# A retention state updated with two heads per matmul, and weight units converted three steps later

## The chip, the cores and the metric

The kernel runs on one core of one Trainium2 chip. The metric is the device time of one execution in microseconds (us); a difference of 0.2% is 1.8 us here.

## The reference

Three stages run one after the other: a retention (attention with a decaying causal mask and no softmax) over 4 batches of 8 heads, 576 positions and 64 features per head; a two-layer block of width 2048 with the Mish activation; and a gated block of width 1536 with SiLU. Everything is float32.

```python
def _attn_ref(q, k, v):                       # (4, 8, 576, 64) each
    scores = scale * np.matmul(q, k.transpose(0, 1, 3, 2))
    gamma = 1.0 - 2.0 ** (-5.0 - np.arange(H, dtype=np.float32))
    Dmat = np.where(rel >= 0, gamma[:, None, None] ** rel[None, :, :], 0.0)
    return np.matmul(scores * Dmat[None], v)
...
x = attn_out.transpose(0, 2, 1, 3).reshape(B * S, H * D)    # (2304, 512)
h = x @ moe_w_in;  x = (h * np.tanh(np.log1p(np.exp(h)))) @ moe_w_out
g = x @ moe2_w_gate
out = (g * sigmoid(g) * (x @ moe2_w_val)) @ moe2_w_out
```

## The kernel before, in words

**Retention** (`retention`, L309 to L627) takes 20 steps: four batches, each cut into four pieces of 128 positions and a last one of 64 (`sc` counts the pieces, `nsc` is 5). The heads lie in four pairs (`NP`), `e` is the head within its pair. A step `t` is written out by hand, and every engine works through its instructions in the written order. On TensorE a step is: `inter` (L517), queries times the running state, into `o0` for the first 64 positions and `o1` for the second; `scores` (L457, in the short last piece L446); `state(t, 1)` (L498); `transposes(t + 1)` (L410, of the next keys); the matmuls of a slot of the next stage, in four of the steps; `products` (L530), the masked scores times the scaled values; `state(t + 1, 0)`; and `q_ahead`, transposes of queries (L379, in one step of five L372). The rows of the matmuls have 64 partitions and 64 columns: the float32 operands of the heads are laid on four quarters of the array (64 rows by 64 columns each).

**The state.** After each half `c` of 64 positions, `state(t, c)` adds k times v of that half to a state that stays in PSUM (`stp`, one tile per batch). For each of the eight heads there is one matmul of 64 by 64, which writes to the head's own half of the partitions; ScalarE then copies the state to SBUF (`sbd`, L507, 128 partitions by 256 elements), from where `inter` takes it as weights. There are 32 such updates (four batches, four full pieces, two halves).

**Around it.** ScalarE also copies the transposes out of PSUM (L381, L374, L412), VectorE masks the scores (L471) and scales the outputs into `x` (L540), GpSimd scales v (L427). Loads of k, v and q run four to six steps ahead (`load`, `load_q`).

**Weight units.** Each pair of weight blocks of the Mish layers is loaded raw (`fetch`, 512 KB) and turned into a high and a low part: `rebias_raw` (L106, L107), `sign` (L111), `join` (L115), `part` (L121 on ScalarE, L122 on GpSimd in retention and on VectorE after it). `conversions` yields these as pieces, in this order: rebias 0, sign 0, rebias 1, join 0, sign 1 with part 0, rebias 2, and so on. In retention `zeroth.one()` takes one piece per step from step 3 on (L611) and one more in each step listed in `EARLY` (L602). After retention each slot takes pieces worth `RATES[4]` = 3.3 (L740), where a unit's pieces are worth 0.55 + 1.4 + 0.7.

**EARLY slots.** The Mish layer's first four slots run inside retention, at the steps listed in `EARLY`: `g1` (L636, 12 matmuls) there, `mish` and its split one step later. Slots 0 and 1 read unit 0, slots 2 and 3 unit 1. `RATES` and `PREP` set how fast, and from which slot on, the pieces of the last stage's weights are handed out after retention (`second`, `third`).

Of the kernel before, what the change touches and what calls it, by code (L numbers as in the profile page):

```python
# [7 lines left out]
F32 = mybir.dt.float32  # L8
# [8 lines left out]
def retention_mish_swiglu(  # L17
# [17 lines left out]
    nc = tc.nc  # L35
    B, H, S, D = q.shape
# [4 lines left out]
    NP = H // 2  # L41
# [4 lines left out]
    C = 64  # L46
# [1 line left out]
    RAW, XS = 4, 6  # L48
    OFF = 2
    W = (12, 3, 8, 2, 2, 1)  # L50
    PREP = 25
    NC = 4
    RATES, AHEAD = (1.9, 1.2, 1.1, 1.15, 3.3), 45
    EARLY = (9, 11, 14, 17)

    xp = ctx.enter_context(tc.tile_pool(name="xp", bufs=1))
    cr = ExitStack()
# [253 lines left out]
    nsc = -(-S // 128)  # L311

    def retention(g1, mish, g_hi, g_lo):
        with ExitStack() as c0:
# [3 lines left out]
            at = c0.enter_context(tc.tile_pool(name="at", bufs=2))  # L318
            ps1 = c0.enter_context(tc.tile_pool(name="ps1", bufs=1, space=PSUM))
# [8 lines left out]
            sbd = {}  # L328
            qkv = {}
# [32 lines left out]
            qT, kT, vs, pp = {}, {}, {}, {}  # L362
# [23 lines left out]
            def q_cols(t):  # L386
                b, sc, n = steps[t]
                return qT[b, sc // 2][:, :, sc % 2 * 128:sc % 2 * 128 + n]


            def q_ahead(t, half):
                b, sc, n = steps[t]
                due = (
                    ((b, 1, 1),) if b else ((b, 1, 0),),
                    ((b, 2, 0),) if b else ((), (b, 1, 1)),
                    ((b + 1, 0, 0),) if b else ((b + 1, 0, 0), (b, 2, 0)),
                    ((b + 1, 0, 1),),
                    ((b + 1, 1, 0),),
                )[sc]
                if half < len(due) and due[half]:  # L400
                    q_transposes(*due[half])

            def transposes(t):
                if t >= len(steps):
                    return
                b, sc, n = steps[t]
                src = qkv["k", t]
                p = ps1.tile([128, NP, 128], F32, tag="tk", name=f"tk{t}")
                for pr in range(NP):
                    nc.tensor.transpose(p[:, pr, :n], src[:n, 2 * pr:2 * pr + 2, :], ident[:n, :n])  # L410
                kT[t] = at.tile([128, NP, 128], F32, tag="kT", name=f"kT{t}")
                nc.scalar.copy(out=kT[t][:, :, :n], in_=p[:, :, :n])  # L412
# [23 lines left out]
            def scores(t):  # L436
                if t >= len(steps):
                    return
                b, sc, n = steps[t]
                s = ps1.tile([128, 2, 512], F32, tag="s", name=f"s{t}")[:, :, :NP * C]  # L440
                s = s.rearrange("p e (a n) -> p e a n", a=NP)
                sc_[t] = s
                if n == C:
                    for pr in range(NP):
                        for e in range(2):
                            nc.tensor.matmul(  # L446
                                s[64 * e:64 * e + 64, 0, pr, :],
                                lhsT=kT[t][64 * e:64 * e + 64, pr, :C],
                                rhs=q_cols(t)[64 * e:64 * e + 64, pr, :],
                                start=True,  # L450
                                stop=True,
                            )
                    return
                for pr in range(NP):
                    for c in range(n // C):
                        for e in range(2):
                            nc.tensor.matmul(  # L457
                                s[C * c:C * c + C, e, pr, :],
                                lhsT=kT[t][64 * e:64 * e + 64, pr, C * c:C * c + C],
                                rhs=q_cols(t)[64 * e:64 * e + 64, pr, C * c:C * c + C],  # L460
                                start=True,
                                stop=True,
                            )

            def masks(t):
                if t >= len(steps):
                    return
                n, s = steps[t][2], sc_.pop(t)
                r = n // C
                pp[t] = at.tile([128, 2, NP, C], F32, tag="p", name=f"p{t}")  # L470
                nc.vector.tensor_tensor(  # L471
                    out=pp[t][:, :r], in0=s[:, :r],
                    in1=mask.unsqueeze(1).unsqueeze(1).to_broadcast([128, r, NP, C]),
                    op=ALU.mult,
                )
# [10 lines left out]
            stp = {}  # L486
            due = []

            def state(t, c):
                if t >= len(steps) or steps[t][1] == nsc - 1:  # L490
                    return
                b, sc, n = steps[t]
                if (sc, c) == (0, 0):
                    stp[b] = ps1.tile([128, NP, D], F32, tag="st", name=f"state{b}")
                for pr in range(NP):
                    for e in range(2):
                        h = 2 * pr + e
                        nc.tensor.matmul(  # L498
                            stp[b][64 * e:64 * e + 64, pr, :],
                            lhsT=qkv["k", t][C * c:C * c + C, h, :],  # L500
                            rhs=vs[t][C * c:C * c + C, h, :],
                            start=(sc == 0 and c == 0 and pr == 0),
                            stop=(sc == nsc - 2 and c == 1),
                            skip_group_check=True,
                        )
                sbd[t, c] = at.tile([128, NP, D], F32, tag="sbd", name=f"sbd{t}_{c}", bufs=3)
                nc.scalar.copy(out=sbd[t, c], in_=stp[b])  # L507

            outs_ = {}
# [1 line left out]
            def inter(t):  # L511
                b, sc, n = steps[t]
                outs_[t] = [ps1.tile([128, NP, C], F32, tag=f"o{c}", name=f"o{t}_{c}") for c in range(n // C)]
                for c in range(n // C):
                    for pr in range(NP if sc or c else 0):
                        for e in range(2):
                            nc.tensor.matmul(  # L517
                                outs_[t][c][64 * e:64 * e + 64, pr, :],
                                lhsT=sbd[(t, 0) if c else (t - 1, 1)][64 * e:64 * e + 64, pr, :],
                                rhs=q_cols(t)[64 * e:64 * e + 64, pr, C * c:C * c + C],  # L520
                                start=(pr == 0), stop=False, skip_group_check=True,
                            )
# [50 lines left out]
            def warm(n):  # L573
                for _ in range(n):
                    nc.tensor.matmul(idle[:, :128], lhsT=zero, rhs=zero, start=True, stop=True)  # L575
# [10 lines left out]
            for t in range(len(steps)):  # L586
                if t < 2:
                    warm(W[3 + t])
                if t == len(steps) - 1:
                    g1(LAG, (0, KT // 2))  # L590
                inter(t)
                scores(t)
                state(t, 1)
                masks(t)
                transposes(t + 1)
                q_ahead(t, 1)
                warm(W[5] if t < 2 else 0)
                if t == len(steps) - 1:
                    g1(LAG, (KT // 2, KT))
                if t in EARLY:  # L600
                    g1(EARLY.index(t))
                    zeroth.one()  # L602
                products(t)
                state(t + 1, 0)
                q_ahead(t, 0)
                scale(t + 2)
                if t + 1 < nsc:
                    gout_chunk(t + 1)
                if t - 1 in EARLY:
                    mish(EARLY.index(t - 1))  # L610
                if t > 2:  # L611
                    zeroth.one()
                if t - 1 in EARLY:
                    g_hi(EARLY.index(t - 1))
                    g_lo(EARLY.index(t - 1), nc.gpsimd)
                if due:
                    split_x(xt, "x", *due.pop(0), nc.gpsimd)
                load(t + 4, "k", k)
                load(t + 4, "v", v)
                if t == 0:  # L620
                    load_q(4)
                    load_q(5)
                load_q(t + 6)
                if t in (1, 3, 5):
                    fetch()
            splits[0] = nc.vector
            fetch()  # L627
# [1 line left out]
    with tc.manual_schedule():  # L629
# [38 lines left out]
        def g1(s, part_=(0, KT)):  # L668
            b, i = where(s)
            if not part_[0]:  # L670
                hs[s] = bank(s)
            prod(hs[s], unit["in", i], "x", b, part_)
# [44 lines left out]
        def slot(s):  # L717
# [22 lines left out]
            zeroth(RATES[4])  # L740
            if s >= PREP and not (parts and s < 2 * F1):
                third(RATES[3])
# [487 lines left out]
```

## Time and profile before

| | us |
|---|---|
| three runs, median (lowest to highest) | 916.27 (915.99 to 917.32) |
| the profiled execution | 915.34 |
| its span, first to last instruction | 913.6 |
| TensorE busy in the span | 899.7 (98%) |
| VectorE, ScalarE, GpSimd busy | 547.0, 375.9, 47.7 |

What is predicted is the time of the runs; the profiled execution is 0.93 us below their median, and its time is 1.74 us over its span. PE is TensorE's matmuls, PEld its weight loads, which run under other matmuls. A float32 matmul of L498, L517, L457, L530 and L575 leaves two records of each kind, a transpose or a matmul of the later stages one.

### The profile page before, as it was taken

Reading aid. Unit: us, or ns where it says so; the run is one execution under the profiler, and the core shown is the slowest. Engines: PE = TensorE matmul, PEld = TensorE weight load, DVE = VectorE, ACT = ScalarE, POOL = GpSimd, SP = SyncE. Lnnn points to the kernel's source line nnn. Section 1 sums busy time; section 2 is a strip of 40 time slices with the busy share of each in tenths; the row PEclk is TensorE's granted clock in tenths of the full one; section 3 lists DMA queues with packets and bytes.
Section 4 is the critical chain, followed back from the end, with each engine's and each line's share of the span. In section 5 each row is a group of like instructions: output and inputs, shape, how many; then the busy total and the mean of one; then the engine's idle time right before and its main releaser. Section 6 shows DMA issues by size and latency. Waiting matters only on the chain.

```text
span 913.6 us, 17176 instructions
## 1 busy us (share of the span) xinstructions
PE 899.7 (98%) x6810; PEld 840.9 (92%) x6810; DVE 547.0 (60%) x1094; ACT 375.9 (41%) x787; POOL 47.7 (5%) x52
## 2 busy tenths in 40 slices
PE   8899999999999999999999999999999999999998
PEld 8788899999999999999999999999999999999997
DVE  3344487866878784667695666747444556444444
ACT  3665456644655554454464333323222223222222
POOL 2344200000000000000000000000000000000000
PEclk9999999999999999999999999999999999999999
DMA  8997245544787767589859666545644455644421
GB/s 184 240 225 184 71 140 159 164 127 167 248 289 254 263 226 259 165 274 334 280 189 359 194 206 206 174 155 177 204 161 161 162 161 163 215 156 160 160 93 70
DMA packets 125648, 177.68 MB, mean 194 GB/s; under 512 B 47104, under 2 KB 84608, under 8 KB 125568
## 3 DMA queue, kind: packets, MB, share of 16 engines
q1 hardware_dynamic: 124432, 176.45, 61.3%
q8 instruction: 54, 0.88, 0.4%
q10 hardware_dynamic: 1136, 0.13, 0.1%
q14 instruction: 26, 0.21, 0.1%
HBM read 133.04 MB, written 43.52 MB: 193 GB/s over the span
## 4 chain that ended last, share of the span: by engine, by line
PE 95%; DVE 2%; ACT 1%; issue 1%; DMA 1%; SPq 0%; DVEq 0%; ACTq 0%
PE t L887 28%; PE fa L1063 16%; PE h L636 14%; PE ea L925 7%; PE da L925 7%; PE te L887 6%; PE acc L680 6%; PE o L517 2%; PE state L498 2%; PE o L530 1%; PE tk L410 1%; PE idle L575 1%; PE tq L379 1%; PE s L457 1%; PE acc L900 1%
## 5 line engine op out<-in xcount | busy, mean ns | idle before, releaser
L887 PE MATMUL t<-y,su 128*128 128x384 f32 x1512 | 306.5, 338 | 0.5 <-DVE cv L894 0.5
L887 PEld LDWEIGHTS t<-y,su 128*128 128x128 f32 x1512 | 270.7, 188 | 24.2 <-DVE cv L894 1.8
L1063 PE MATMUL fa<-fu,g 128*128 128x512 f32 x648 | 189.9, 395 | 0.1
L636 PE MATMUL h<-xs,u 128*128 128x384 f32 x672 | 127.5, 336 | 0.2 <-ACT m L697 0.2
L1063 PEld LDWEIGHTS fa<-fu,g 128*128 128x128 f32 x648 | 118.4, 188 | 7.6 <-ACT g L1086 0.5
L636 PEld LDWEIGHTS h<-xs,u 128*128 128x128 f32 x672 | 115.6, 188 | 1.7 <-ACT m L697 0.3
L1086 ACT CAST g<-sg 128x384 fp32r<-128x384 f32 x72 | 36.9, 513 | 173.7 <-DVE sg L1122 120.4
L925 PE MATMUL ea<-ge,u 128*128 128x512 f32 (+1 forms) x384 | 76.0, 336 | 0.0
L925 PE MATMUL da<-g,u 128*128 128x512 f32 (+1 forms) x384 | 72.0, 336 | 0.1
L887 PE MATMUL te<-ye,eu 128*128 128x384 f32 x336 | 68.0, 337 | 0.0
L925 PEld LDWEIGHTS ea<-ge,u 128*128 128x128 f32 x384 | 61.8, 188 | 5.9
L925 PEld LDWEIGHTS da<-g,u 128*128 128x128 f32 x384 | 60.4, 188 | 7.1 <-DVE x L540 0.4
L1111 ACT ACTIVATE sg<-sg 128x384 f32<-128x384 f32 x54 | 28.4, 526 | 90.6 <-DVE sg L894 90.6
L1091 DVE TENSOR_TENSOR g<-sg,g 128x384 fp32r<-128x384 f32 x72 | 40.2, 558 | 40.6 <-ACT g L1086 40.6
L680 PE MATMUL acc<-g,u 128*128 128x384 f32 x336 | 63.1, 336 | 0.8 <-DVE y L690 0.8
L710 DVE TENSOR_TENSOR g<-m,g 128x384 fp32r<-128x384 f32 x60 | 33.4, 556 | 46.6 <-ACT g L706 46.6
L680 PEld LDWEIGHTS acc<-g,u 128*128 128x128 f32 x336 | 58.6, 188 | 1.3 <-DVE y L690 1.3
L887 PEld LDWEIGHTS te<-ye,eu 128*128 128x128 f32 x336 | 56.8, 188 | 2.2 <-DVE ve L894 0.3
L697 ACT ACTIVATE m<-h 128x384 f32<-128x384 f32 x64 | 31.4, 490 | 55.3 <-PE h L636 55.0
L894 DVE TENSOR_TENSOR u<-t,p 128x384 f32<-128x384 f32 x36 | 20.0, 556 | 43.3 <-PE t L887 40.8
L894 DVE TENSOR_TENSOR v<-t,p 128x384 f32<-128x384 f32 x36 | 20.0, 556 | 35.6 <-PE t L887 34.9
L706 ACT CAST g<-m 128x384 fp32r<-128x384 f32 x64 | 32.9, 513 | 1.8
(131 smaller groups left out, 1039.6 us busy)
## 6 DMA issues: line engine op xcount, KB each, us to landing
su<-comb SPq DMA_DIRECT2D x126, 512.0 KB, 3.3
comb<-c SPq DMA_DIRECT2D x84, 256.0 KB, 2.6
eu<-ecomb SPq DMA_DIRECT2D x28, 512.0 KB, 4.6
raw<-in_moe_w_in_dram SPq DMA_DIRECT2D x16, 512.0 KB, 3.7
raw<-in_moe_w_out_dram SPq DMA_DIRECT2D x16, 512.0 KB, 3.7
ecomb<-e_s SPq DMA_DIRECT2D x32, 256.0 KB, 2.3
rawg<-in_moe_w_gate_dram SPq DMA_DIRECT2D x12, 512.0 KB, 6.1
ecomb<-u SPq DMA_DIRECT2D x24, 256.0 KB, 4.0
```

Source lines behind the costliest of these rows:

```text
L636: nc.tensor.matmul(ps, lhsT=u[:, a, kk * 128:(kk + 1) * 128], rhs=s[:, e, :], start=(c == 0), stop=(c == n - 1),)
L680: nc.tensor.matmul(accs[b][d][:, :T], lhsT=u[:, a, d * 128:(d + 1) * 128], rhs=g[:, e, :], start=(i == 0 and c == 0), stop=(i == F1 - 1 an ...
L697: nc.scalar.activation(w, hs.pop(s), AF.Mish)
L706: nc.scalar.copy(out=gs[s][:, 0, :], in_=ws[s])
L710: eng.tensor_tensor(out=g[:, 1, :], in0=ws.pop(s), in1=g[:, 0, :].bitcast(F32), op=ALU.subtract)
L887: nc.tensor.matmul(p, lhsT=w[:, a, kk * 128:(kk + 1) * 128], rhs=y[kk][:, x, :], start=begin and kk == 0 and (a, x) == (0, 0), stop=kk == ...
L894: nc.vector.tensor_tensor(out=out_, in0=a, in1=b_, op=ALU.add)
L925: nc.tensor.matmul(o, lhsT=u[:, a, d * 128:(d + 1) * 128], rhs=y[:, :512] if r == 0 else y[:, 512:], start=f == 0 and (a, x) == (0, 0) and ...
L1063: nc.tensor.matmul(accs["f", b][m], lhsT=gs[u, e, h][:, x, m * 128:(m + 1) * 128], rhs=fu[2 * (u % PAIRS) + e][:, a, :], start=first, stop ...
L1086: nc.scalar.copy(out=gs[u, e, h][:, 0, :], in_=x)
L1091: nc.vector.tensor_tensor(out=g[:, 1, :], in0=x, in1=g[:, 0, :].bitcast(F32), op=ALU.subtract)
L1111: nc.scalar.activation(x, bank_ if part_ is None else x, AF.Silu)
```

## The change

The state tile gets a full bank of PSUM, 128 columns per pair of heads. `state` takes both heads of a pair at once: the weights are the keys of both (64 rows by 128 columns), the moving operand is the values of both (128 columns), and the result holds the two heads' states on its diagonal and two products of unlike heads beside it, which nothing reads. The copy to `sbd` takes the whole bank, 128 by 512 elements, and `inter` reads the diagonal blocks. The pieces of the weight units start at step 6 instead of 3, the three raw loads of the loop come at steps 4, 6 and 8 instead of 1, 3 and 5, and the EARLY slots stand at steps 11, 13, 15 and 17 instead of 9, 11, 14 and 17. `PREP` and two of the `RATES` are a little higher.

```diff
--- before.py
+++ after.py
@@ -48,10 +48,10 @@
     RAW, XS = 4, 6
     OFF = 2
     W = (12, 3, 8, 2, 2, 1)
-    PREP = 25
+    PREP = 26
     NC = 4
-    RATES, AHEAD = (1.9, 1.2, 1.1, 1.15, 3.3), 45
-    EARLY = (9, 11, 14, 17)
+    RATES, AHEAD = (1.95, 1.2, 1.15, 1.15, 3.3), 45
+    EARLY = (11, 13, 15, 17)
 
     xp = ctx.enter_context(tc.tile_pool(name="xp", bufs=1))
     cr = ExitStack()
@@ -491,19 +491,17 @@
                     return
                 b, sc, n = steps[t]
                 if (sc, c) == (0, 0):
-                    stp[b] = ps1.tile([128, NP, D], F32, tag="st", name=f"state{b}")
+                    stp[b] = ps1.tile([128, NP, 128], F32, tag="st", name=f"state{b}")
                 for pr in range(NP):
-                    for e in range(2):
-                        h = 2 * pr + e
-                        nc.tensor.matmul(
-                            stp[b][64 * e:64 * e + 64, pr, :],
-                            lhsT=qkv["k", t][C * c:C * c + C, h, :],
-                            rhs=vs[t][C * c:C * c + C, h, :],
-                            start=(sc == 0 and c == 0 and pr == 0),
-                            stop=(sc == nsc - 2 and c == 1),
-                            skip_group_check=True,
-                        )
-                sbd[t, c] = at.tile([128, NP, D], F32, tag="sbd", name=f"sbd{t}_{c}", bufs=3)
+                    nc.tensor.matmul(
+                        stp[b][:, pr, :],
+                        lhsT=qkv["k", t][C * c:C * c + C, 2 * pr:2 * pr + 2, :],
+                        rhs=vs[t][C * c:C * c + C, 2 * pr:2 * pr + 2, :],
+                        start=(sc == 0 and c == 0 and pr == 0),
+                        stop=(sc == nsc - 2 and c == 1),
+                        skip_group_check=True,
+                    )
+                sbd[t, c] = at.tile([128, NP, 128], F32, tag="sbd", name=f"sbd{t}_{c}", bufs=3)
                 nc.scalar.copy(out=sbd[t, c], in_=stp[b])
 
             outs_ = {}
@@ -516,7 +514,7 @@
                         for e in range(2):
                             nc.tensor.matmul(
                                 outs_[t][c][64 * e:64 * e + 64, pr, :],
-                                lhsT=sbd[(t, 0) if c else (t - 1, 1)][64 * e:64 * e + 64, pr, :],
+                                lhsT=sbd[(t, 0) if c else (t - 1, 1)][64 * e:64 * e + 64, pr, 64 * e:64 * e + 64],
                                 rhs=q_cols(t)[64 * e:64 * e + 64, pr, C * c:C * c + C],
                                 start=(pr == 0), stop=False, skip_group_check=True,
                             )
@@ -608,7 +606,7 @@
                     gout_chunk(t + 1)
                 if t - 1 in EARLY:
                     mish(EARLY.index(t - 1))
-                if t > 2:
+                if t > 5:
                     zeroth.one()
                 if t - 1 in EARLY:
                     g_hi(EARLY.index(t - 1))
@@ -621,7 +619,7 @@
                     load_q(4)
                     load_q(5)
                 load_q(t + 6)
-                if t in (1, 3, 5):
+                if t in (4, 6, 8):
                     fetch()
             splits[0] = nc.vector
             fetch()
```

TensorE, step 7 of retention (`s` is the scores, `state` the running state, `tk` the transposed keys, `o_0` and `o_1` the two outputs; the numbers are the tiles'), before:

```order
L457 MATMUL s_958<-qT_1_724,kT_890 64x64 x16
L498 MATMUL state_712<-vs_824,k_668 64x64 x8
L410 MATMUL tk_987<-ident,k_737 128x128 x4
L530 MATMUL o_0_940<-p_985,vs_824 64x64 x2
L530 MATMUL o_1_941<-p_985,vs_824 64x64 x2
```

and the same step after the change:

```order
L457 MATMUL s_900<-qT_1_682,kT_833 64x64 x16
L496 MATMUL state_674<-vs_775,k_632 128x128 x4
L410 MATMUL tk_925<-ident,k_694 128x128 x4
L528 MATMUL o_0_882<-p_923,vs_775 64x64 x2
L528 MATMUL o_1_883<-p_923,vs_775 64x64 x2
```

The update keeps its place and becomes four matmuls of double width in both directions; nothing else of the step moves.

TensorE, the first EARLY slot (`h`, from the unit `u_1033`, which is unit 0), before, in step 9, the short one of the second batch:

```order
L379 MATMUL tq_0_1_1115<-ident,q_741 128x128 x4
L517 MATMUL o_0_1135<-qT_2_926,sbd_1_1086 64x64 x8
L446 MATMUL s_1144<-qT_2_926,kT_1095 64x64 x8
L410 MATMUL tk_1155<-ident,k_934 128x128 x4
L636 MATMUL h_1162<-xs_0_573,u_1033 128x384 x3
```

and after, in step 11 (unit 0 is `u_1203` there):

```order
L379 MATMUL tq_1_1_1193<-ident,q_878 128x128 x4
L515 MATMUL o_0_1211<-qT_0_957,sbd_1_1157 64x64 x8
L515 MATMUL o_1_1212<-qT_0_957,sbd_0_1191 64x64 x8
L457 MATMUL s_1229<-qT_0_957,kT_1166 64x64 x16
L496 MATMUL state_1100<-vs_1115,k_970 128x128 x4
L410 MATMUL tk_1254<-ident,k_1056 128x128 x4
L634 MATMUL h_1261<-xs_0_543,u_1203 128x384 x3
```

The slot moves from a short step to a full one.

ScalarE, where the high part of unit 0 is made (`CAST u`), before, in the tail of step 7, two steps ahead of its slot:

```order
L507 COPY sbd_0_1020<-state_712 128x256
L381 COPY qT_0_1023<-tq_0_0_1022 64x512 x2
L121 CAST u_1033<-raw_471 128x512
L295 CAST xs_1_1036<-x_650 128x384
L507 COPY sbd_1_1086<-state_712 128x256
```

and after, in the tail of step 10:

```order
L505 COPY sbd_0_1191<-state_1100 128x512
L381 COPY qT_1_1108<-tq_1_1_1193 64x512 x2
L121 CAST u_1203<-raw_700 128x512
L505 COPY sbd_1_1250<-state_1100 128x512
L412 COPY kT_1259<-tk_1254 128x512
```

The piece now stands one step ahead of the slot that reads it, and the copies of the state are twice as wide.

## Rows read from the trace of the kernel before

**Rows 1.** The page's chain of work that ended last, shares of the span.

```profile
PE 95%; DVE 2%; ACT 1%; issue 1%; DMA 1%; SPq 0%; DVEq 0%; ACTq 0%
```

**Rows 2.** Busy time per stretch: us, engines with instruction counts, PEclk, DMA share, GB/s.

```profile
0.00:110.00 110.00, 101.28 (x2465) 90.47 (x2466) 45.44 (x87) 58.40 (x118) 41.84 (x44) 0.98 0.80 183
110.00:220.00 110.00, 110.00 (x637) 103.53 (x636) 80.27 (x152) 61.37 (x117) 0.00 (x0) 1.00 0.50 152
220.00:914.00 694.00, 688.38 (x3712) 646.87 (x3710) 421.26 (x857) 256.09 (x553) 5.83 (x8) 1.00 0.61 203
```

**Rows 3.** The chain of work in order of time (start us, us, what), 13 to 74.

```profile
13.98 0.45 PE state L498 x16
...
15.02 0.45 PE idle L575 x4
...
16.19 0.72 issue
...
46.95 0.84 issue
...
73.33 1.45 issue
```

**Rows 4.** TensorE in order of time, steps 6 and 7: start us, us, what, count.

```profile
41.40 1.08 PE L517 MATMUL o<-qT,sbd 64*64 64x64 f32 x29
...
44.00 0.69 PE L530 MATMUL o<-p,vs 64*64 64x64 f32 x32
44.51 0.63 PE L498 MATMUL state<-vs,k 64*64 64x64 f32 x16
45.08 0.46 PE L372 MATMUL tq<-ident,q 64*128 64x64 f32 x4
45.46 1.08 PE L517 MATMUL o<-qT,sbd 64*64 64x64 f32 x29
```

**Rows 5.** Groups of 0 to 134 us by shape: busy us, mean ns, idle before.

```profile
L498 PE MATMUL state<-vs,k 64*64 64x64 f32 x512 | 22.3, 219 | 2.2 <-issue 2.2
L507 ACT COPY sbd<-state 128x256 f32<-128x256 f32 x32 | 11.9, 372 | 33.6 <-PE state L498 33.5
L412 ACT COPY kT<-tk 128x512 f32<-128x512 f32 x16 | 9.4, 588 | 4.8 <-PE tk L410 4.6
```

**Rows 6.** Timeline at step 5, where `inter` follows its copy.

```profile
37.60 0.54 PEld L517 LDWEIGHTS o<-qT,sbd 64*64 64x64 f32 x15 [0.17 <-ACT sbd L507]
```

**Rows 7.** Timeline at the end of the stop ahead of `inter` in step 4.

```profile
32.99 1.12 PE L517 MATMUL o<-qT,sbd 64*64 64x64 f32 x16 [2.02 <-ACT raw L106]
32.99 0.93 PEld L517 LDWEIGHTS o<-qT,sbd 64*64 64x64 f32 x15 [1.84 <-issue]
```

**Rows 8.** Stretches from stop to stop, and the slow one; columns as in Rows 2.

```profile
26.40:32.95 6.55, 4.51 (x126) 3.92 (x126) 2.58 (x4) 4.63 (x10) 3.01 (x3) 0.97 1.13 270
47.75:52.85 5.10, 4.47 (x127) 3.86 (x126) 2.05 (x4) 3.17 (x7) 0.24 (x1) 1.00 0.93 208
32.55:35.95 3.40, 2.96 (x37) 2.51 (x37) 0.42 (x1) 0.77 (x2) 2.01 (x2) 0.50 0.93 185
```

**Rows 9.** DMA queues: packets, MB, share of 16 engines; whole span.

```profile
q8 instruction: 54, 0.88, 0.4%
```

**Rows 10.** Timeline from the making of unit 0 to its first use.

```profile
50.30 0.66 PE L379 MATMUL tq<-ident,q 128*128 128x128 f32 x4
52.14 0.65 ACT L121 CAST u<-raw 128x512 fp32r<-128x512 f32 x1
52.87 1.29 POOL L122 TENSOR_TENSOR u<-raw,u 128x512 fp32r<-128x512 f32 x1 [4.87 <-ACT u L121]
57.06 1.12 PE L636 MATMUL h<-xs,u 128*128 128x384 f32 x5
```

**Rows 11.** Timeline: the eighth unit's low part, and its first matmuls.

```profile
115.47 0.69 DVE L122 TENSOR_TENSOR u<-raw,u 128x512 fp32r<-128x512 f32 x1
...
124.77 1.43 PE L925 MATMUL da<-g,u 128*128 128x512 f32 x7
```

## The prediction

> **What bounds the kernel now.** I read the page first. Of the chain of work that ended last, 95% is TensorE [rows 1], so an instruction added to TensorE adds its time unless TensorE would have stood still there. The second view is the busy time by stretch. The change lies in the first 110 us, where TensorE is busy for 101.3 us: 8.7 us of standing still is the most that longer instructions could fill. From 110 to 220 us it never rests, and in all the rest it lacks 5.6 us [rows 2]. The third view is the chain in order of time through retention. It is TensorE's own work, piece after piece, with stops put down to "issue" between them, of 0.72, 0.71 (at 25.75), 0.84, 0.65 (at 52.26) and 1.45 us, 4.4 us together [rows 3]. A sixth stop, of 2.0 us, is put down to ScalarE's `raw` piece, but the weight loads of the same matmuls waited 1.84 us for "issue" [rows 7]. I hold it to be of the same kind: from the stop before it to its end TensorE has 126 matmuls and 126 loads, and between the next two such stops 127 and 126 [rows 8]; with the few semaphore instructions that makes 256 each time. The instruction queue moved 0.88 MB in 54 packets [rows 9], 16 KB each, and 16 KB over 256 is 64 bytes. So the program of TensorE comes in blocks of 256 instructions, and six of them came late, while loads of q, k and v filled the DMA engines (0.93 and 1.13 of their time [rows 8]). [...]
>
> **The update itself.** Before, an update is eight matmuls in 16 records, which the chain charges 0.45 us [rows 3]; by their starts, 44.51 to 44.92 and one pair's pace more, they take 0.47 [rows 4, 5]. I take 0.46. Two of them, on different columns of the array, run side by side. After, it is four matmuls in 8 records, each over all columns, with 128 moving columns instead of 64. The nearest row is the idle matmul of 128 by 128 by 128: four records in 0.45 us, 0.112 each [rows 3]. All four matmuls of one update sit on the same 64 rows, so I see nothing that could run side by side: 8 x 0.112 = 0.90 us. That is 0.44 us more, 32 times: **+14.1 us**. The bounds: 0.112 is 128 moving columns at full clock and I see no row above it at that clock; below it stands the pace of today's records, 0.46 / 16 = 0.029 us, which is the rival at the other end.
>
> **Changes of shape.** From `products` to `state` the shape stays at 64 by 64: the last record of L530 starts at 44.00 + 0.69 - 0.22 = 44.47 (a record lasts 0.22 [rows 5]), the first of L498 at 44.51, 0.04 later. From `state` to the wider transposes it changes: 44.51 + 0.63 - 0.22 = 44.92 to 45.08, 0.16 later, against 0.06 from pair to pair inside an update [rows 4]. A change so costs 0.10 us. The way out of the update changed shape already; the way in now does too, in all but the first of the 32, which follows idle matmuls: 31 x 0.10 = **+3.1 us**. No row shows a matmul of 64 rows by 128 columns behind one of 64 by 64; the lower bound is 0, and I take 3.1, since both neighbours that change width pay it.
>
> **The wider copy.** Of 256 elements it takes 372 ns, and a copy of 512 from PSUM 588 ns [rows 5]: 0.22 more, 6.9 us over 32 on an engine busy for 58.4 of 110 us [rows 2]. On TensorE's path it stands only where little lies between an update and the `inter` that reads it. At the head of a batch the loads wait 0.17 us for it today [rows 6], and will wait 0.22 longer: three times 0.22. At steps 2 and 18 no transposes lie between, and 0.2 each is left over. **+1.1 us**, from 0 to 2. Elsewhere 0.6 us of transposes and half of `inter` cover it; without them each copy would cost its 0.22.
>
> **What it gives back.** A full step has 136 matmul records today (32 in each of `inter`, `scores` and `products`, 32 in two updates, 8 in transposes), with as many loads 272 instructions, in 45.46 - 41.40 = 4.06 us [rows 4]. A block of 256 thus lasts 3.8 us. After, a step has 240 instructions and lasts 4.06 + 2 x 0.54 = 5.1 us, a block 5.5 us. If a block comes as late after the one before as now, each stop shrinks by up to 1.7 us: five vanish, of the longest 0.3 stays. I book **-5.9 us** of the 6.4 (they are 4.4 and 2.0). Bounds: 0, if the fetch is late whatever TensorE does, and all 8.7 us of standing still. With the 2.0 us stop gone, its slow stretch should go: **-1.7 us**, or 0.
>
> [...]
>
> **What is moved.** Three 512 KB raw loads leave steps 1, 3 and 5 for 4, 6 and 8. On SP's queue the loads of q, k and v between them go ahead of them, and those run four to six steps ahead; DMA is 1% of the chain [rows 1], so I book nothing. Three pieces (0.55 + 1.4 + 0.7 = 2.65 in the units of which a slot hands out 3.3) go from retention to the slots, which makes each unit 0.8 of a slot later, some 3.3 us (a slot is 24 matmuls, of 110 / 637 us each [rows 2]). Cover: the unit with the least slack is ready at 116.16 and first read at 124.77 [rows 11]; without it each us beyond 8.6 would stop TensorE. The EARLY slots only stand elsewhere. The one place with no slack is the first: unit 0 was ready 3.86 us after the first transpose of the tail it is made in (54.16 - 50.30), with 2.9 us to spare [rows 10]. Now its slot comes one step later, not two: after a step less `products` and an update, 4.06 - 1.08 + 0.54 = 3.5 us [rows 4], and the third matmul, the first to read the low part, a third of a us behind: 3.86 again. I book 0, and up to GpSimd's 1.3 us. `PREP` and `RATES` shift VectorE's work under a TensorE that hardly waits: 0, up to 1 either way.
>
> **Sum.** 14.1 + 3.1 + 1.1 - 5.9 - 1.7 = +10.7 us. The profiled execution took 915.34, so 926.0; the median of the runs shown is 0.93 above it, so **927.0 us**.
>
> **The rivals.** First, the stops stay: the blocks come late because the DMA engines are full, and that holds for a longer step if its loads come as thickly. For it: the DMA share of 0.93 to 1.13. Against: the same bytes over a longer time, and stops only in some blocks, in front of short records. Then 14.1 + 3.1 + 1.1 = +18.3, **934.6 us**. Second, TensorE's standing still takes up all it can and shapes cost nothing: 14.1 - 8.7 - 1.7 = +3.7, **920 us**. Against it: the change of shape shows in rows 4 at a width that the new matmul shares. Third, on the other side: TensorE pays per record and not per column. Then 8 records take 8 x 0.029 = 0.23 us and an update gains 0.23, 7.4 us in all; shapes and copies cost 4.2 and the stops give 1.3 (a block then lasts about 0.25 us longer): -4.5, **911.8 us**. It decides below about 0.048 us a record. For it: records start every 0.029 us now. Against: the idle matmuls, 0.112 at the same clock, and that two of today's run at once. Between 0.045 and 0.055 us a record nothing would be measured, within 0.2% (1.8 us, what a measurement here can tell from no change).
>
> **How the numbers follow.** The forecast 0.66, with 922 to 932 of its own; the stops stay 0.18; all absorbed 0.09; paid per record 0.04; no change 0.03. So faster 0.04, same 0.03, slower 0.93. The range goes from all absorbed, 920, to the stops staying, 935, which leaves out about 0.15; the u0 wait and the copies' 2 us could take it past that.
>
> **What would show it.** Right: in the changed kernel an update is charged about 0.9 us in the chain, on 8 records; a gap of 0.15 us lies ahead of its first record; "issue" within retention falls to about half a us; no stretch below full clock after the start; retention ends some 10 us later, and everything behind it keeps its length. Wrong: updates charged 0.5 us or less; "issue" of 4 us or more; a wait of the first EARLY slot for GpSimd above a us, or a new wait between 110 and 220 us.

## The result, and the profile after

The changed kernel takes 927.65 us (median of 4 runs, 927.33 to 927.95); the kernel before, run beside it, 916.80 us (915.99 to 917.70). The ratio is 1.0136, with a 95% interval from 1.0110 to 1.0162: slower by 10.9 us. The profiled execution took 927.95 us with a span of 926.2, against 915.34 and 913.6 before. The ratios here and below leave out runs more than 1.5% above the fastest of their kernel, which are three of six of `e6` and one of six of `e8`.

First the page of the changed kernel: its span, TensorE's busy time, the chain of work that ended last, and the instruction queue (packets, MB, share).

```profile
span 926.2 us, 16648 instructions
PE 916.9 (99%) x6554; PEld 854.6 (92%) x6554; DVE 549.7 (59%) x1095; ACT 382.0 (41%) x787; POOL 45.8 (5%) x51
PE 92%; DVE 4%; ACT 2%; DMA 1%; issue 1%; SPq 0%; DVEq 0%; ACTq 0%
q8 instruction: 52, 0.85, 0.4%
```

A kernel can become slower and its main engine busier at once: what is new is work, not waiting. The busy time by stretch says where (columns as in [rows 2]); the first row ends where the first `da` matmul of the chain starts, and behind it stands the same row of the kernel before, in which that matmul starts at 108.25.

```profile
0.00:118.96 118.96, 116.32 (x2199) 102.60 (x2200) 42.16 (x81) 63.01 (x115) 39.99 (x43) 1.00 0.71 164
122.00:232.00 110.00, 110.00 (x636) 103.48 (x635) 80.70 (x151) 61.03 (x115) 0.00 (x0) 1.00 0.47 144
232.00:927.00 695.00, 687.54 (x3705) 645.74 (x3703) 423.94 (x860) 256.69 (x556) 5.81 (x8) 1.00 0.62 205
```

```profile
0.00:108.25 108.25, 99.53 (x2455) 88.89 (x2455) 43.69 (x84) 58.03 (x117) 41.84 (x44) 0.98 0.80 184
```

Up to `da` TensorE is busy 16.8 us longer (116.32 for 99.53) and stands still 6.1 us less (2.64 for 8.72): 10.7 us later. Then 110 us without a rest, as before. In the last 695 us it lacks 7.46 us where it lacked 5.62 [rows 2]: 1.8 us. Both together are the 12.6 us between the spans.

The chain of work of the changed kernel (start us, us, what) has 1.08 us for an update of 8 records where [rows 3] have 0.45 for 16. No piece of "issue" over 0.1 us is left in it.

```profile
46.05 0.63 PE o L528 x32
46.67 1.08 PE state L496 x8
47.76 0.24 PE tq L372 x4
48.00 1.10 PE o L515 x29
...
112.87 0.58 ACT sbd L505
113.45 0.28 ACT kT L412
113.73 0.41 ACT m L695
114.18 1.32 PE h L634 x6
...
118.96 2.13 PE da L923 x11
```

### The profile page after: what moved, and what is told of

Same layout as the page of the kernel before. It is cut to its first block, busy times and chain, and to the rows that moved or that the text cites. A ratio compares the mean times of both kernels' runs of the same rounds, so it can differ in the third digit from the quotient of the medians.

```text
span 926.2 us, 16648 instructions
## 1 busy us (share of the span) xinstructions
PE 916.9 (99%) x6554; PEld 854.6 (92%) x6554; DVE 549.7 (59%) x1095; ACT 382.0 (41%) x787; POOL 45.8 (5%) x51
## 4 chain that ended last, share of the span: by engine, by line
PE 92%; DVE 4%; ACT 2%; DMA 1%; issue 1%; SPq 0%; DVEq 0%; ACTq 0%
PE t L885 28%; PE fa L1061 16%; PE h L634 13%; PE da L923 7%; PE ea L923 6%; PE te L885 6%; PE acc L678 5%; PE state L496 4%; PE o L515 2%; PE o L528 1%; PE idle L573 1%; PE tk L410 1%; PE s L457 1%; PE acc L898 1%; PE tq L379 1%; DMA rawv<-in_moe_w_val_dram 1%
## 5 line engine op out<-in xcount | busy, mean ns | idle before, releaser
L496 PE MATMUL state<-vs,k 64*128 64x128 f32 x256 | 37.0, 285 | 0.0
```

The costliest lines, as they stand in the source:

```text
L496: nc.tensor.matmul(stp[b][:, pr, :], lhsT=qkv["k", t][C * c:C * c + C, 2 * pr:2 * pr + 2, :], rhs=vs[t][C * c:C * c + C, 2 * pr:2 * pr + 2 ...
```

## The experiments

Each kernel was timed in turns with the kernel before on the same chip. The kernel before spreads over 7 us (910.5 to 917.3 in one set of 17 runs); versions without stops, of four or five runs each, over 0.6 to 2.3, but `e3` and `e9`, which have stops, over 1.7 and 1.8 too. So each set has its own median of before: 914.89 (first four kernels), 914.59 (next four), 912.11 (`e9`, `e10`) and 914.61 (`e11`, `e12`).

My theory: the update costs some 17 us of TensorE's time with the changes of shape, and its longer blocks of 256 instructions end the stops. Rivals for the second half: the later raw loads end them; any longer step does; the smaller number of instructions does.

**The parts apart.** e1: the update and its copy alone, everything else as before:

```diff
-    PREP = 26
+    PREP = 25
...
-    RATES, AHEAD = (1.95, 1.2, 1.15, 1.15, 3.3), 45
-    EARLY = (11, 13, 15, 17)
+    RATES, AHEAD = (1.9, 1.2, 1.1, 1.15, 3.3), 45
+    EARLY = (9, 11, 14, 17)
...
-                if t > 5:
+                if t > 2:
...
-                if t in (4, 6, 8):
+                if t in (1, 3, 5):
```

> The wide update and the whole-bank copy alone; the pieces, raw loads, EARLY slots, PREP and RATES stand as before. Theory (the wide update makes a block of 256 TensorE instructions last 5.5 us instead of 3.8, so the blocks are no longer late): the six stops of 6.4 us and the slow-clock stretch are gone without any of the shifts; 926.3 us, 1.3 below the changed kernel, since the wait at 305 us belongs to the shifts. Rival (the raw loads in steps 1 to 5 made the blocks late, and moving them cured it): at least 3 us of stops stay, 930 us or more.

It took 925.41 us (924.97 to 925.95), ratio 1.0122 [1.0102, 1.0142]: 10.5 us slower. No stop of "issue" over half a us, no slow clock behind the start, `da` at 118.00. So the update by itself both costs and cures.

e2: the other half alone, the shifts with the update of before (the same lines the other way round, in the kernel before):

> The shifts alone (pieces from step 6, raw loads at 4, 6, 8, EARLY 11, 13, 15, 17, PREP and RATES), with the narrow update of before. Theory: a block lasts 3.8 us as before, stops of 4 to 8 us stay, and the wait of 1.3 us at 305 us comes; 916 to 919 us. Rival (the raw loads made the blocks late): the stops fall below 2 us and the slow-clock stretch goes, about 911 us.

It took 917.79 us (12 runs), ratio 1.0033 [1.0017, 1.0050], 2.9 us slower than before. The stops are there. First two pieces of its chain, then three stretches of its busy time (columns as in [rows 2]; the granted clock is the third number from the end):

```profile
42.33 2.40 issue
...
65.08 1.39 issue
```

```profile
44.70:51.50 6.80, 6.76 (x149) 6.30 (x151) 1.97 (x5) 2.66 (x6) 1.57 (x2) 0.62 0.99 241
32.00:35.40 3.40, 3.30 (x51) 2.85 (x52) 0.42 (x1) 0.57 (x1) 1.96 (x2) 0.59 0.93 194
66.40:69.80 3.40, 3.33 (x48) 2.89 (x52) 0.14 (x1) 1.87 (x4) 0.00 (x0) 0.55 1.00 264
```

This profile is of the slowest of its runs (921.35 us), with three slow stretches where [rows 8] had one. The raw loads' place does not end the stops.

e4: the changed kernel with `PREP` and `RATES` of before:

```diff
-    PREP = 26
+    PREP = 25
...
-    RATES, AHEAD = (1.95, 1.2, 1.15, 1.15, 3.3), 45
+    RATES, AHEAD = (1.9, 1.2, 1.1, 1.15, 3.3), 45
```

> The changed kernel with PREP and RATES of before. Theory: the new wait of 1.3 us for VectorE at 305 us comes from VectorE's work handed out faster there, and goes; 926.3 us. Rival: it comes from the three pieces that left retention, and stays; 927.6 us.

925.48 us (925.18 to 926.25), ratio 1.0124 [1.0103, 1.0144]. That is `e1`'s time within 0.1 us: the raw loads, the three pieces and the EARLY slots are worth nothing under the wide update. e5: the changed kernel itself once more, unedited, in the next set, which ran on another chip:

> The changed kernel as it is, timed beside the others of this group. Theory (PREP and RATES cost the wait at 305 us and a little behind it): 1.3 to 2 us above the version with the old PREP and RATES, 926.8 to 927.7 us. Rival (the two differ by the state of the chip alone): 925.5 us.

927.41 us (925.99 to 928.32), ratio 1.0137 [1.0116, 1.0158]. Against `e4`, `PREP` and `RATES` cost 1.9 us by the medians of the two chips, 1.7 by the profiled spans (926.2 and 924.5) and 1.2 by the ratios, whose intervals overlap. The timelines show where: in the changed kernel TensorE waits for VectorE's last `xs` at 305.03, and in `e4` the same matmuls run through.

```profile
305.03 2.17 PE L634 MATMUL h<-xs,u 128*128 128x384 f32 x11 [1.26 <-DVE xs L300]
```

```profile
302.17 4.33 PE L634 MATMUL h<-xs,u 128*128 128x384 f32 x24
```

In the trace of `e5` the same wait is 1.88 us, at 304.97, and behind it stand 3.4 us at half clock, from 306.28. Whether the wait brought them is not shown: behind the 1.26 us of the changed kernel's trace the clock stays full.

**What ends the stops.** e3: the update of before, done twice, the second time into a half of the bank that nothing reads: as much TensorE time as the change adds, but 16 more matmuls in a step, in 32 records.

```diff
...
+                for again in range(2):
...
-                            stp[b][64 * e:64 * e + 64, pr, :],
+                            stp[b][64 * e:64 * e + 64, again, pr, :],
```

> The kernel before with every narrow update done twice, the second time into another part of the bank that nothing reads: as much more TensorE time per step as the wide update costs (32 x 0.47 = 15 us), but 32 more records per step instead of 16 fewer. Theory (what counts is how long 256 instructions last: 336 instructions in 5.0 us, 3.8 us a block as before): the stops stay, 5 to 9 us of them, 931 to 934 us. Rival (a longer step alone cures the stops, since the loads then come thinner): no stops and no slow clock, 923.5 us.

930.21 us, ratio 1.0171 [1.0150, 1.0192]; the stops stay. The longest in its chain, and the stretch of half clock that begins within it:

```profile
47.92 3.21 issue
```

```profile
49.40:56.20 6.80, 5.07 (x100) 4.83 (x101) 0.07 (x1) 1.16 (x3) 1.57 (x2) 0.50 0.50 104
```

The longer step with more instructions did not cure here. Its step has 336 instructions in about 5.0 us, so its block still lasts 3.8 us. The time of a block and number of instructions were told apart by making the update longer with few, wide matmuls: one added pair of 256 columns (e9, without the outer loop), or three (e11).

```diff
...
+                for again in range(3):
+                    for e in range(2):
+                        nc.tensor.matmul(
+                            stp[b][64 * e:64 * e + 64, 1],
+                            lhsT=qkv["k", t][C * c:C * c + C, e, :],
+                            rhs=vs[t][C * c:C * c + C, :NP, :],
+                            start=False, stop=(sc == nsc - 2 and c == 1), skip_group_check=True,
+                        )
...
```

> The kernel before, with one pair of matmuls more in each update: 64 by 64 weights, 256 moving columns, into the other half of the state's bank, which nothing reads. The added pair is four records (and four weight loads) of 256 columns, two at a time on the two halves of the rows, so about 0.43 to 0.46 us an update by the pace of 64-column records today, some 14 us in all. That is the time which the wider update added, but the number of instructions in a step does not fall: it rises from 272 to 288. A step takes 4.06 + 2 x 0.45 = 4.96 us, a block of 256 instructions 4.4 us instead of 3.8. Theory (a block comes some us after the last, whatever TensorE does with the instructions; each stop shrinks by what the block got longer): stops of about 0.6 us each less, 2 to 3 of the 6.4 us left, 925 to 928 us. Rival one (it is the number of TensorE's instructions that brings the stops, not their time): the stops stay at 6 us or more, 930 us and above. Rival two (any longer update ends them): no stop over half a us, 921 to 923 us.

928.03 us (926.72 to 928.54), ratio 1.0169 [1.0149, 1.0189]: 15.9 us slower than before. The stops are there, 6.9 us of them; its chain has

```profile
32.31 0.96 issue
...
39.17 1.21 issue
...
58.80 1.92 issue
```

My expectation of 2 to 3 us left was wrong; the stops stayed, as the first rival had it. Then e11, three pairs:

> The kernel before with three added pairs of 256-column matmuls in each update instead of one (again into the half of the bank that nothing reads). Three times 0.43 us an update, 32 updates: +41.3 us. A step has 320 TensorE instructions in 4.06 + 2 x 1.29 = 6.64 us, so a block of 256 lasts 5.3 us, as in the changed kernel (5.4), though the number of instructions in a step is higher and not lower. If the length of a block decides (the stops end somewhere between 4.4 us, where they were still all there, and 5.4): no stop over half a us, against the same call's kernel before +41.3 - 6.4 - 1.7 = +33.2 us. If it is the number of short matmuls in a row that decides: stops of 6 us or more stay, +39 to +42 us.

947.18 us (946.58 to 947.60), ratio 1.0363 [1.0336, 1.0389]: +32.6 us, where the block's length had said +33.2. No stop is left, with 320 instructions in a step, more than any kernel with stops but `e3`. Its chain shows the added pairs (L508) and no issue between them:

```profile
28.53 0.41 PE state L498 x14
28.94 1.36 PE state L508 x12
30.30 0.59 PE tk L410 x4
```

e12: the wide update in the first half of each step only:

```diff
...
+                if c == 0:
                     for pr in range(NP):
                         nc.tensor.matmul(
                             stp[b][:, pr, :],
...
+                else:
+                    for h in range(2 * NP):
+                        r = slice(64 * (h % 2), 64 * (h % 2) + 64)
+                        nc.tensor.matmul(
+                            stp[b][r, h // 2, r],
...
```

> The wide update alone (nothing moved, whole bank copied) in the first half of each step, the update of before, eight pairs of 64 by 64, in the second half, into the diagonal blocks that inter reads. A step has 256 instructions in 4.06 + 0.54 = 4.6 us, a block lasts 4.6 us. Update and change of shape cost half of the whole change: 7.0 + 1.6, the copies 1.1: +9.7 us before what the stops give back. If the length of a block decides and the edge lies below 4.6 us: no stops, 9.7 - 6.4 - 1.7 = +1.6 us against the kernel before. If it lies above: stops of 5 us or more, +7 to +10 us. If each stop shrinks by what a block got longer: about 2.5 us of stops left, +4 us.

918.99 us (918.16 to 920.28), ratio 1.0061 [1.0038, 1.0084]: +4.4 us. Two stops are left, 1.8 us, and its clock stays full behind the start. Of its three branches the third comes nearest (about 2.5 us of stops left, +4 us):

```profile
38.08 0.68 issue
...
43.96 0.64 issue
```

The profiles that bear on the stops, in one table, one trace each. A stop is counted here where the starts of two matmuls behind each other lie over 0.5 us apart, from 13 us to where retention's last two steps begin; the length of a block is 256 by the time of a full step over its instructions. For the last two columns TensorE's records (matmuls, weight loads, semaphore instructions) are counted in order of time: a stop is at a block's end when the number of records ahead of it is 192 above a multiple of 256, within two.

| kernel | TensorE instructions in a step | block, us | stops | at a block's end | sum of these, us |
|---|---|---|---|---|---|
| before | 272 | 3.8 | 7 | 6 | 7.8 |
| `e7` (below) | 272 | 3.8 | 7 | 6 | 7.7 |
| `e2` | 272 | 3.8 | 5 | 3 | 6.5 |
| `e3` | 336 | 3.8 | 7 | 6 | 7.7 |
| `e9` | 288 | 4.4 | 6 | 6 | 6.9 |
| `e12` | 256 | 4.6 | 2 | 2 | 1.8 |
| `e11` | 320 | 5.3 | 0 | 0 | 0 |
| changed, `e1`, `e4`, `e5` | 240 | 5.5 (changed) | 0 | 0 | 0 |

The last column goes with the block's length (but for `e2`), not with the number of instructions. The prediction's six are the six of before at a block's end, behind records 448, 960, 1214, 1984, 2240 and 3264. The seventh, 1.00 us at 21.62, stands behind record 689, where no block ends; the chain comes through ScalarE's `qT` there, and the changed kernel still has 0.41 us of it.

The instruction queue agrees with late blocks as the cause. It moved as many 16 KB packets as 256 goes into TensorE's records: 54 for 13,831 before, 52 for 13,319 in the changed kernel, 58 for 14,855 in `e3`, 57 for 14,599 in `e11`. Each of the six stops of before, with the time when TensorE entered the block ahead of it (us):

```
block entered   packet starts   next block starts   behind the packet
11.39           14.06           16.91               2.85
21.85           23.79           26.46               2.67
26.46           30.34           32.99               2.65
42.73           45.45           47.79               2.34
47.79           50.42           52.91               2.49
69.90           71.90           74.78               2.88
```

A packet started 1.9 to 3.9 us after the block ahead was entered, and its instructions ran 2.3 to 2.9 us after that; in these six TensorE stood still where the block's own work was shorter than the two together (in the second, 3.68 us of work against 1.94 and 2.67). The other 12 crossings of before, up to 103 us, cost at most 0.33 us each.

**Loads nearer to their use.** e7: if the loads of k and v only crowd the fetch because they come early, they may come a step later:

```diff
...
-                load(t + 4, "k", k)
-                load(t + 4, "v", v)
+                load(t + 3, "k", k)
+                load(t + 3, "v", v)
```

> The kernel before with the loads of k and v three steps ahead instead of four. Theory (blocks are late because the fetch queues behind loads in flight): fewer loads are in flight, the stops fall by 1 to 4 us, 911 to 914 us, unless a load then comes late. Rival (the DMA engines are full whatever the depth): stops as before, 915 us; or TensorE waits for loads, above 916.

913.74 us (12 runs), ratio 0.9991 [0.9967, 1.0016]: no difference, and the stops stay.

**Two ways to a cheaper change.** e6 keeps the update of before, and makes `inter` one matmul for two heads, with 128 by 128 block-diagonal weights and 64 moving columns, hoping for half its records at today's pace; its blocks are copied by ScalarE and VectorE.

```diff
+                for e in range(2):
+                    (nc.scalar.copy, nc.vector.tensor_copy)[e](
+                        out=sbd[t, c][64 * e:64 * e + 64, :, 64 * e:64 * e + 64], in_=stp[b][64 * e:64 * e + 64]
+                    )
...
+                        nc.tensor.matmul(
+                            outs_[t][c][:, pr, :],
+                            lhsT=sbd[(t, 0) if c else (t - 1, 1)][:, pr, :],
+                            rhs=q_cols(t)[:, pr, C * c:C * c + C],
```

> The kernel before, its narrow update kept, with inter as one matmul per pair and half on a block-diagonal state (128 rows by 128 columns, 64 moving columns): half of inter's instructions in the same 0.45 us; the state is copied in two halves, by ScalarE and VectorE. A step has 240 instructions instead of 272 in about 4.06 us, a block lasts 4.3 us instead of 3.8. Theory: each stop is about 0.5 us shorter, 2 to 3 us in all, 911 to 914 us. Rival (the stops have nothing to do with the number of instructions, and the two copies cost): 915 us or more.

A clear miss: 959.53 us (median of six, 945.59 to 960.71), ratio 1.0430 [1.0373, 1.0486]; its profiled run had TensorE at half clock for 48 us from 36.1, so I read e8, the same with the loads of `e7`.

> The last two together. Theory: 909 to 913 us. Rival: 915 us or more.

950.10 us (median of six, 944.83 to 959.18), ratio 1.0385 [1.0348, 1.0422]. Three things went wrong. In its chain, at full clock, 16 of the new records take 1.73 us, their starts 0.112 us apart, where 29 of today's take 1.08 [rows 4]; the second fence is its list of waits (waiter, releaser, us in total, times, longest).

```profile
30.25 1.73 PE o L522 x16
...
33.11 0.38 ACT sbd L511
...
33.51 0.43 DVE sbd L511
...
33.95 0.70 DVE p L473
```

```profile
DVE sbd L511 <- ACT sbd L511: 40.4, 21, 3.0
...
PE o L535 <- DVE p L473: 14.6, 14, 1.2
```

And VectorE's half of the copy starts when ScalarE's has ended; the mask piece `p` stands behind it in VectorE's queue, and `products` wait for it. Third, its trace has 20.5 us at half clock, in four stretches between 36.8 and 135.8: up to 10 of its 35 us, if all work takes twice as long there, as 16 of the new records do in `e6` (3.31 us at 50.90, in its 48 us at half clock).

e10 splits the wide copy between the two engines, in `e1`:

```diff
-                nc.scalar.copy(out=sbd[t, c], in_=stp[b])
+                nc.scalar.copy(out=sbd[t, c][:, :2], in_=stp[b][:, :2])
+                nc.vector.tensor_copy(out=sbd[t, c][:, 2:], in_=stp[b][:, 2:])
```

> The wide update alone (nothing moved, the planner's numbers of before), with its whole-bank copy split into two halves of 256 columns, the first by ScalarE, the second by VectorE at the same time. Theory (at the head of a batch and in steps 2 and 18 the end of the copy stands on TensorE's path, 1 to 2 us in all, and nothing else of the copy counts): the loads of inter no longer wait for the copy, 923.5 to 924.5 us where the wide update alone with the one copy took 925.4. Rival (VectorE's half waits behind its masks, or the masks behind it, and what TensorE saved at the copy it loses there): 925.4 or more, with waits for VectorE in retention.

942.66 us, ratio 1.0329 [1.0309, 1.0350]: the rival's direction, and 30.5 us over before (up to 3.4 of them from 6.8 us at half clock), where `e1` had 10.5. The timeline has the same row of events: 0.37 us of copy on ScalarE, then VectorE's, then the mask, then `products`.

```profile
21.46 0.37 ACT L505 COPY sbd<-state 128x256 f32<-128x256 f32 x1 [2.46 <-PE state L496]
...
21.87 0.42 DVE L506 COPY sbd<-state 128x256 f32<-128x256 f32 x1 [2.14 <-ACT sbd L505]
...
22.21 0.68 DVE L471 TENSOR_TENSOR p<-s,mask 128x512 f32<-128x512 f32 x1
...
22.95 0.29 PE L529 MATMUL o<-p,vs 64*64 64x64 f32 x4 [0.27 <-DVE p L471]
```

The two copies never lay side by side (VectorE waited for ScalarE's copy 32 times of 32). Why is open: both read one state tile and write one `sbd` tile, and no run tried two.

## Why the prediction was right

927.0 was forecast, 927.65 measured, and the retention's end moved by 10.7 us, the sum to the tenth. Part of that is luck: errors that cancel. For sizes I add up the chain's pieces from 6 us to the first `da`, before and after.

**The update, +14.1, and the shapes, +3.1: 16.3 together.** The chain's `state` pieces grow from 15.2 to 33.5 us, 18.3 more; the `tk` pieces shrink by 1.9: 16.3 in all, 0.9 under the sum of 17.2. A full step takes 42.76 to 47.93, 5.17 us, for 4.06 in [rows 4]: 1.11 more, 1.08 forecast. The timeline of TensorE:

```profile
42.76 1.08 PE L515 MATMUL o<-qT,sbd 64*64 64x64 f32 x29
...
44.30 1.16 PE L496 MATMUL state<-vs,k 64*128 64x128 f32 x8
45.39 0.66 PE L410 MATMUL tk<-ident,k 128*128 128x128 f32 x4
...
47.93 1.17 PE L515 MATMUL o<-qT,sbd 64*64 64x64 f32 x29
```

From the first record of an update to the next piece it is 1.09 us now and 0.63 (42.78 to 43.41) before; the rest is the way in. Within an update the starts lie 0.112 us apart. So the idle matmul of the same width was the right row, and the rival that TensorE pays per record is out. Whether the 0.112 us comes from the 128 moving columns or from the weights' 128 is not shown: in `e8`, 64 moving columns under such weights take it too. The shape term was rough in two ways. The way in measured 0.15 us against 0.04 before, as booked. But where the 64-row `tq` follows the update, both are of 64 by 128 now and nothing is paid (47.60 for `tq`'s first start is 1.00 behind the update's, where a 128-row piece comes 1.08 behind). And what I did not see at all: at the four short steps the `tk` transposes of 64 rows run between the records of the update, on the other half of the rows, as this timeline of the changed kernel shows:

```profile
31.61 0.27 PE L410 MATMUL tk<-ident,k 64*128 64x64 f32 x1
31.71 0.27 PE L496 MATMUL state<-vs,k 64*128 64x128 f32 x1
31.72 0.28 PE L410 MATMUL tk<-ident,k 64*128 64x64 f32 x2
31.82 0.27 PE L496 MATMUL state<-vs,k 64*128 64x128 f32 x1
```

That saves about 0.4 us each, 1.6 of the 1.9. My sentence that I saw nothing that could run beside an update held for the update's own matmuls only.

**The wider copy, +1.1: about 1.0, in the places named and one more.** By form, up to 122 us (busy us, mean ns, idle before it and its releasers):

```profile
L496 PE MATMUL state<-vs,k 64*128 64x128 f32 x256 | 37.0, 285 | 0.0
L505 ACT COPY sbd<-state 128x512 f32<-128x512 f32 x32 | 18.7, 586 | 44.0 <-PE state L496 44.0
L515 PEld LDWEIGHTS o<-qT,sbd 64*64 64x64 f32 x512 | 17.0, 134 | 4.3 <-ACT sbd L505 1.4 <-issue 1.1 <-ACT kT L412 0.5
```

A copy takes 586 ns (588 forecast); loads of `inter` wait 1.4 us for it, at five places in the chain, the three heads of a batch and steps 2 and 18; before, these waits came to 0.5. In the chain `sbd` grows by 3.2 us where `tq`, which it stands in for, shrinks by 2.2. Not seen was the one in the chain above at 112.87: ScalarE's own queue. Copy, `kT` and `m` stand behind each other there, and the `h` matmul waits 0.72 us for `m`, 0.2 before.

**The stops, −5.9, and the slow clock, −1.7: the stops right in size, the clock half, and the step to the stops not borne out.** "issue" falls from 5.0 to 0.9 us in the chain, and the ScalarE pieces that stood there for the 2.0 us stop go, `qT` of 1.23 us and `raw` of 0.66 (31.01 to 32.93): 6.0 in all. (By my own figures, 6.4 less the 0.3 that I left of the longest, I should have booked 6.1.) The clock is full from 6.21 to 924.39 us. The 1.7 that I booked for the slow stretch, my estimate of half of its 3.4 us at 0.50 [rows 8], no run shows: the chain's `o` and `s` pieces got 0.8 shorter. The cause held: `e1` shows that the wide update alone ends the stops, `e11` that a block of 5.3 us ends them with more instructions too. My rule for it, each stop shorter by what the block got longer, is not borne out: at 4.4 us (`e9`) each should have lost 0.6 and of 7.8 us only 0.9 went, at 4.6 (`e12`) three quarters were gone, and of the longest, for which I left 0.3, nothing stayed. It said "if a block comes as late after the one before as now", and that condition failed: at the stops the packet started 1.9 to 3.9 us behind the entry into the block ahead before, 1.4 to 4.3 in `e9`, 4.0 and 2.9 in `e12`. With that scatter and one trace each, an edge between 4.4 and 5.3 us can't be told from a slope. What makes a packet start late is open; that the loads of q, k and v do was argued from the profile, `e7` moved them without effect, and no run took them away.

In the traces with blocks of 5.3 us and more no crossing of a block in retention costs over half a us. With 3.8 us, of the 18 crossings of before between 16 and 103 us, six cost 7.8 us.

**The moved pieces, 0: right.** `e4` and `e1` are 0.1 us apart. Unit 0's first slot took 2.24 us at 70.23 where the one at 93.27 took 2.09, of the 1.3 us that it could have cost; all `h` pieces together are 0.3 longer.

**`PREP` and `RATES`, 0 and up to 1 either way: wrong, +1.2 to 1.9.** `e4` without them is faster by that much, by ratio or by median; from the first `da` on the changed kernel's trace is 1.8 us longer than that of `e4`. The 1.26 us wait for `xs` at 305 is theirs (the matmul starts 1.6 us behind the one before it, where they follow each other 0.17 apart). `e2` has the same wait, 0.91 us at 298.42, with the update of before.

**What filled the hole.** Retention came out at 10.7 because the misses cancel: update and shapes 0.9 less than summed, `x` and `kT` pieces that left the chain 0.6 less, against 0.9 less from the slow clock, 0.4 for the start (full clock at 6.21 us for 5.24, in no term) and the 0.3 of `h`. The 1.8 us of `PREP` and `RATES` did show: the profiled execution took 927.95 us where the sum had 926.0. It is not seen in the forecast, since I had added 0.93 for a median above its profile, and the changed kernel's median lies 0.30 below: luck again.

No version was measured faster than the kernel before. The end of the stops is worth about 6.8 us (6.0 in the chain, 0.8 of slow clock), but the wide update is an expensive way to it, at 16 us. `e12` buys most of it for half the price and still loses 4.4 us.

## What to carry to other kernels

Two matmuls of 64 by 64 that ran side by side on the array were not made cheaper by one of double width: half of the products are thrown away, and an update of half as many records took 1.09 us for 0.63. Count instructions against time as well: here "issue" stops that lay multiples of 256 instructions apart, 7.8 us before, stood where a packet of the instruction queue had started 2.3 to 2.9 us earlier, and the work that ended them looked cheaper than it was, by about 6.8 us. Split a copy between two engines only after a look at who else stands in the second one's queue: in `e10` `products` waited 14.4 us in all for the masks, which stand behind VectorE's copy.

## What was not expected of the hardware

- Records with 128 by 128 weights and 64 moving columns came 0.11 us apart (16 in 1.73 us in `e8`), like those of 128 columns with weights as wide (four in 0.45 us [rows 3]). Half the columns saved nothing.
- In the changed kernel a 64-row transpose and a 64-row update on the other half of the rows ran between each other, their records started 0.01 to 0.10 us apart (31.61 to 31.82), though one has 64 moving columns and the other 128.
- The stops at block ends went with the block's length: 3.8 us, 6.5 to 7.8 us of stops in four kernels; 4.4 us, 6.9; 4.6 us, 1.8; 5.3 us and above, none. Before, up to 103 us, no block began sooner than 2.3 us behind the start of its packet.
- TensorE's clock was at half about some stops: for 3.4 us about the end of the 2.0 us stop of before, for 6.8 us about that of 3.21 us in `e3`. About others it was not: `e9`, with a stop of 1.92 us, shows full clock throughout retention. In `e5` 3.4 us of it followed a wait of 1.88 us for VectorE, at 305 us.
